# The last 64-row tile of FFN-down: two half passes of adjacent sums as 64-row tiles in the two halves of the array

## The chip, the cores and the metric

The kernel runs on one core of a Trainium2 chip. A core has TensorE (PE in the profile; its weight loads are PEld), VectorE (DVE), ScalarE (ACT), GpSimd (POOL) and SyncE (SP), which here only issues DMAs. The metric is device time in microseconds of one execution, the median of several.

## The reference

The inputs are x (2 x 4096 tokens x 640), two sets of small block weights, a gate vector and the weights of a gated feed-forward net. What is computed, in float32:

```python
g = sigmoid((x * gate_w).sum(-1, keepdims=True))
a = irfft(block_mlp(rfft(x, over the 4096 tokens)))   # complex, 4 blocks of 160, ReLU, soft shrinkage
b = (gelu(x @ w_gate) * (x @ w_up)) @ w_down          # 640 -> 1728 -> 640
out = g * a + (1 - g) * b
```

The change lies in the product with `w_down` (1728 x 640), called FFN-down here, at the end of the kernel.

## The kernel before

**Split numbers.** Operands of TensorE are in a float32 form that keeps fewer bits. To keep the accuracy, a value x is held as a high part (`high`, line 268, a ScalarE copy that rounds) and a low part (`low`, line 271, a VectorE subtraction x - high). A product of two split values is three passes: high x high, low x high and high x low; low x low is left out.

**The stages.** First come the gate and up products, with the forward transform put in between (to about 1440 us of the span), then the block MLP in the frequency domain, and last FFN-down with the inverse transform, from about 1883 us on. FFN-down goes in 32 steps. A step handles two tiles of 128 tokens, n1 and n2 (`toks`), and adds into them what `inv2` computes, 12 passes on line 287 (24 in a few steps).

**A step of FFN-down.** `down` (lines 1086 to 1132) computes the 2 x 2 block product of a pair of token tiles (rows) and two halves of the inner dimension (columns) with the four quarters of `w_down` in the Strassen-Winograd way, with seven products in place of eight. Each is called `blk(a_, b_)`: a11 x b11, s2 x t2, s3 x t3, s1 x t1, a12 x b21, a22 x t4, s4 x b22, in this order. An accumulator is a PSUM bank; A, E, B, C and Dd are different ones, A and E take two products each.

The inner dimension 1728 is 13.5 tiles of 128. Each half has seven tiles; in the second half the seventh (j == 6) has only 64 rows. The products whose left side comes from that half, or whose weights do, are listed in `HALF`. For these the last tile takes two passes, not three:

```python
ops += [(hh, wh), (hh, wl)] if j == 6 and a_ in HALF else [(hh, wh), (hl, wh), (hh, wl)]
```

Here rows 0 to 63 of `hh` hold the high part of the 64 rows and rows 64 to 127 their low part; `wh` holds the high part of the weights twice, so the first pass is high x high and low x high in one. `wl` holds the low part of the weights in rows 0 to 63 and zeros in rows 64 to 127, so the second pass is high x low with half of its rows idle. A step has 4 products of 21 passes and 3 of 20, 144 in all, each with a load of 128 columns of weights (the stationary side is the left operand, `ho`) and a stream of 320 columns. All of them are on line 458 (`run`).

**Preparing the operands.** `h_op` (line 1046) makes the split left side `ho` of one product: ScalarE copies the first five tiles (128x640) and the last two (128x256), VectorE subtracts. For a name in `HALF` the subtraction of the last two is a 128x128 and a 64x128, the latter written to rows 64 to 127. `down` calls the functions in `hooks` between its products: hook k prepares, for k = 0 to 4, the left sides of s3, s1, a12, a22 and s4 of this step, two or more products ahead of their use, and hooks 5 and 6 those of a11 and s2 of the next. ScalarE writes a buffer again only when TensorE has read it. The sums on GpSimd (`h_s3`, `h_s2`, `h_s1`) and the loads for the next step are in the hooks too. The order on each engine is the program's order; nothing is rescheduled.

**Preparing the weights.** `wd_pre` computes the seven forms of the weights once, during the gate and up products; `form` splits each, stores it to DRAM (`wdf`), and `wd_load` brings it back for FFN-down.

Of the kernel before, what the change touches and what calls it, by code (L numbers as in the profile page):

```python
# [10 lines left out]
F32 = mybir.dt.float32  # L11
# [4 lines left out]
P = 128  # L16
# [196 lines left out]
def spectral_mix_kernel(ctx: ExitStack, tc: tile.TileContext, a):  # L213
    nc = tc.nc
    out = a["out"]

    def dr(t, off, ap):
        return bass.AP(tensor=t.tensor, offset=t.offset + off, ap=ap)
# [7 lines left out]
    def bank():  # L226
        return psum.tile([P, 512], F32, name="bank", tag="bank")

    def big(shape, dt=F32, name="big"):
        return pool.tile(shape, dt, name=name, tag="big", bufs=18)  # L230
# [4 lines left out]
    def small(shape, dt=F32, name="small"):  # L235
        return pool.tile(shape, dt, name=name, tag="small", bufs=17)

    def tiny(shape, dt=F32, name="tiny"):
        return pool.tile(shape, dt, name=name, tag="tiny", bufs=21)
# [4 lines left out]
    def st(dst, src):  # L244
        late.append((dst, src))
# [21 lines left out]
    def high(dst, src, scale=1.0):  # L267
        nc.scalar.activation(dst, src, AF.Copy, scale=scale)  # L268

    def low(dst, src, hi, eng=nc.vector):  # L270
        eng.tensor_sub(dst, src, hi.bitcast(F32))  # L271

    def split(dst_h, dst_l, src, eng=nc.vector):

        high(dst_h, src)
        low(dst_l, src, dst_h, eng)
# [179 lines left out]
    def run(dst, ops, first=True):  # L456
        for i, (l, r) in enumerate(ops):
            nc.tensor.matmul(dst, l, r, start=first and i == 0, stop=i == len(ops) - 1, skip_group_check=True)  # L458
# [446 lines left out]

    V, WM, S2, HR, HO = {}, {}, {}, {}, {}
    HALF = ("a12", "a22", "s4", "b21", "t4", "b22")
    c_seq = [(b, na) for b in range(2) for na in range(16)]  # L910
# [10 lines left out]
    def wd_raw(t):  # L921
        raw = RAW["d", t] = small([P, D], name="draw")
        if t < NPAIR:
            ld(raw, a["wd"][t * P:(t + 1) * P])
        else:
            nc.gpsimd.memset(raw[64:], 0.0)
            ld(raw[:64], a["wd"][t * P:])
# [5 lines left out]
    def wd_pre(j):  # L933
        o = {}
        pair = (j, j + 6) if j < 6 else (12, 13)

        def loads():
            for t in pair:
                wd_raw(t)

        def sums(k):
            def f():
                if not o:
                    r1, r2 = (RAW.pop(("d", t)) for t in pair)
                    o.update(b11=r1[:, :320], b12=r1[:, 320:], b21=r2[:, :320], b22=r2[:, 320:])
                n, p, q = (("t1", "b12", "b11"), ("t2", "b22", "t1"), ("t3", "b22", "b12"), ("t4", "b21", "t2"))[k]
                if k % 2 == 0:
                    o["x"] = small([P, 2, 320], name="wx")
                o[n] = o["x"][:, k % 2]
                nc.vector.tensor_sub(o[n], o[p], o[q])  # L950
            return f

        def form(n):
            def f():
                w = small([P, 2, 320], F32R, name="wf")
                if j == 6 and n in HALF:
                    x = o[n][:64]
                    nc.gpsimd.memset(w[64:, 1].bitcast(F32), 0.0)
                    split(w[:64, 0], w[:64, 1], x)
                    high(w[64:, 0], x)  # L960
                else:
                    split(w[:, 0], w[:, 1], o[n])
                st(dr(wdf[j], 640 * FORMS.index(n), [[14 * 320, P], [1, 640]]),
                   w.rearrange("p h d -> p (h d)").bitcast(F32))
            return f
        return [loads], [sums(0), sums(1), form("t1"), form("b21")], [sums(2), sums(3), form("t2"), form("b11"),
                                                                      form("t3"), form("t4"), form("b22")]
# [78 lines left out]
    def h_op(i, name, eng=nc.vector):  # L1046
        t = big([P, 5, 2, P], F32R, name="ho")
        uh, ul = (tiny([P, 2, P], F32R, name="ho") for k in range(2))
        src, six = HR[i].pop(name) if name in ("s1", "s3", "s4", "a22") else HR[i][name]
        split(t[:, :, 0], t[:, :, 1], src, eng)  # L1050
        high(uh, six)
        if name in HALF:
            low(ul[:, 0], six[:, 0], uh[:, 0], eng)
            low(uh[64:, 1], six[:64, 1], uh[:64, 1], eng)
        else:
            low(ul, six, uh, eng)
        HO[i, name] = [(t[:, j, 0], t[:, j, 1]) for j in range(5)] + [(uh[:, j], ul[:, j]) for j in range(2)]

# [27 lines left out]
    def down(i, u, hooks):  # L1086
        b, na = c_seq[i]
        n1, n2 = toks(na)
        g1, g2 = gs[:, b, 1, n1:n1 + 1], gs[:, b, 1, n2:n2 + 1]
        u1, u2 = u[n1], u[n2]  # L1090
        c1, c2 = slice(0, 320), slice(320, 640)
        acc = lambda: bank()[:, :320]

        def blk(a_, b_):
            h = HO.pop((i, a_))
            ops = []
            for j, (hh, hl) in enumerate(h):
                wh, wl = WM[j][b_]
                ops += [(hh, wh), (hh, wl)] if j == 6 and a_ in HALF else [(hh, wh), (hl, wh), (hh, wl)]
            return ops  # L1100
        hooks[0]()
        e = small([P, 2, 320], name="e")
        A = acc()
        run(A, blk("a11", "b11"))
        nc.scalar.activation(e[:, 0], A, AF.Copy)
        hooks[1]()
        B = acc()
        run(B, blk("s2", "t2"))
        nc.vector.tensor_add(e[:, 0], B, e[:, 0])
        hooks[2]()  # L1110
        C = acc()
        run(C, blk("s3", "t3"))
        nc.vector.tensor_add(e[:, 1], C, e[:, 0])
        hooks[3]()
        E = acc()
        run(E, blk("s1", "t1"))
        for x in (E, e[:, 1]):
            nc.vector.scalar_tensor_tensor(u2[:, c2], x, g2, u2[:, c2], op0=OP.mult, op1=OP.add)
        hooks[4]()
        run(A, blk("a12", "b21"), first=False)  # L1120
        nc.vector.scalar_tensor_tensor(u1[:, c1], A, g1, u1[:, c1], op0=OP.mult, op1=OP.add)
        hooks[5]()
        Dd = acc()
        run(Dd, blk("a22", "t4"))
        nc.vector.tensor_add(e[:, 1], Dd, e[:, 1])
        nc.vector.scalar_tensor_tensor(u2[:, c1], e[:, 1], g2, u2[:, c1], op0=OP.mult, op1=OP.add)
        st(out[b, n2], u2)
        hooks[6]()
        run(E, blk("s4", "b22"), first=False)
        nc.vector.tensor_add(e[:, 0], E, e[:, 0])  # L1130
        nc.vector.scalar_tensor_tensor(u1[:, c2], e[:, 0], g1, u1[:, c2], op0=OP.mult, op1=OP.add)
        st(out[b, n1], u1)
# [66 lines left out]
    for k, (b, n2) in enumerate(a_seq):  # L1199
        i, j = steps_a[k]  # L1200
# [31 lines left out]
    for i, key in enumerate(keys):  # L1232
# [16 lines left out]
        for j, t in enumerate(quads):  # L1249
# [10 lines left out]
            n = len(late)  # L1260
# [27 lines left out]
    def events(i, j):  # L1288
        for f, *args in todo.get((i, j), []):
            f(*args)  # L1290
    wl = lambda part, *js: [(wd_load, j, part) for j in js]
# [9 lines left out]
           S - 3: [(v_load, 1), *wl(2, 2)],  # L1301
           S - 2: [(h_load, 0, 0), *wl(1, 2), (h_load, 0, 1), (wd_later,)],
           S - 1: [(c_split, 0), (h_op, 0, "a11"), *wl(1, 3, 4, 5), *wl(0, 6), (h_s3, 0, nc.gpsimd), (h_s2, 0, nc.gpsimd), (c_load, 1)],
           S: [(h_op, 0, "s2"), (c_split, 1), (h_s1, 0, nc.gpsimd)],
           S + 1: [*wl(2, 3), (flush,), *wl(2, 4), (wd_later,)]}
    for i in range(S + 2):
# [16 lines left out]
        if 0 <= i - 1 < S:  # L1323
            b, c, n = steps[i - 1]
# [8 lines left out]
    for i in range(len(c_seq)):  # L1333
        n = i + 1 if i + 1 < len(c_seq) else None
# [3 lines left out]
        def step(k):  # L1338
            def f():
                if (i, k) == (0, 0):  # L1340
                    wd_load(5, 2)
                    wd_later()
                if (i, k) == (0, 2):
                    ahead.update(inv2(1))
                if k in (0, 5):
                    flush()
                if k < 5:
                    if k == 0:
                        h_s4(i)
                    h_op(i, ("s3", "s1", "a12", "a22", "s4")[k])  # L1350
                if n is not None:
                    if k in (1, 2):
                        h_load(n, k - 1)
                    if k == 2 and n > 1:
                        c_load(n)
                        v_load(n)
                    if k == 4:
                        h_s3(n, nc.gpsimd)
                        h_s2(n, nc.gpsimd)
                    if k == 5:  # L1360
                        h_op(n, "a11")
                        if n > 1:
                            c_split(n)
                    if k == 6:
                        h_op(n, "s2")
                        h_s1(n, nc.gpsimd)
            return f
# [23 lines left out]
```

## Time and profile before

| | |
|---|---|
| median of 3 runs | 2622.28 us (2621.71 to 2625.66) |
| the profiled execution | 2621.81 us, span 2620.0 us |
| TensorE busy | 2601.1 us (99%) |
| VectorE, ScalarE, GpSimd busy | 2056.4, 1488.1, 378.2 us |
| passes of FFN-down (line 458, `bank<-wx,ho`) | 4608, busy 681.5 us |

Lines such as `L458 PE MATMUL bank<-wx,ho 128*128 128x320 f32 x4608 | 681.5, 309 | 0.0` name the source line, the engine, the operation, the tiles written and read, the rows and columns of the array in use (128*128), the shape of the stream, the count, the busy time in us, the mean length of one in ns, and the engine's idle time just before them with what ended it. Because matmuls overlap in the array, the length of one (309 ns) is more than the distance from one to the next. A row of a timeline holds the start, the length from the first start to the last end of a merged run, and in brackets the idle time before it with what ended it. A row of the windows view holds the stretch, its length, and for each engine the busy time with the count of instructions, then the granted clock of TensorE (1.00 is full), the share of the DMA engines and GB/s.

### The profile page before, as it was taken

The page shows a single profiled execution, that of the slowest core. Times are in us where ns is not written, and L with a number is a line of the kernel's source. Part 1 is how long each engine was busy: PE and PEld are TensorE (multiplying, and loading weights), DVE is VectorE, ACT ScalarE, POOL GpSimd, SP SyncE. Part 2 cuts the span into 40 slices and gives each one's busy share as a digit, 9 for nine tenths or more (in the row PEclk, how much of TensorE's full clock was granted, in tenths as well). Part 3 has the DMA queues.
Part 4 walks back from the last instruction along what each step waited for, and adds up shares of the span by engine and source line. Part 5 has one row for each costly group of instructions (what it writes and reads, how often), then busy time and mean ns, then how long its engine had stood idle before and what let it go on. Part 6 is the DMA issues. An engine that isn't in the chain of part 4 may idle for free. (4 is left out here: it accounts for less than half of the span.)

```text
span 2620.0 us, 54180 instructions
## 1 busy us (share of the span) xinstructions
PE 2601.1 (99%) x20308; PEld 2590.4 (99%) x20308; DVE 2056.4 (78%) x4223; ACT 1488.1 (57%) x3501; POOL 378.2 (14%) x377
## 2 busy tenths in 40 slices
PE   9999999999999999999999999999999999999999
PEld 9999999999999999999999999999999999999999
DVE  7656567777677777777756788787899999899998
ACT  5444445665555556666645777787744444444443
POOL 0000000000000000000002011111143333333332
PEclk9999999999999999999999999999999999999999
DMA  6454457676667577767766354457944444444442
GB/s 215 165 185 168 175 186 223 206 226 198 214 202 249 167 244 234 238 209 228 229 210 218 115 153 150 129 164 218 309 159 151 135 137 139 151 151 151 144 133 96
DMA packets 341659, 483.10 MB, mean 184 GB/s; under 512 B 24652, under 2 KB 214092, under 8 KB 341396
## 3 DMA queue, kind: packets, MB, share of 16 engines
q1 hardware_dynamic: 325844, 438.15, 52.9%
q0 software_dynamic: 15552, 41.49, 4.5%
q8 instruction: 160, 2.62, 0.4%
q14 instruction: 103, 0.84, 0.1%
HBM read 299.90 MB, written 179.64 MB: 183 GB/s over the span
## 5 line engine op out<-in xcount | busy, mean ns | idle before, releaser
L458 PE MATMUL bank<-xo,w 128*128 128x256 f32 x11736 | 1414.1, 281 | 8.8 <-ACT xo L268 4.9
L458 PEld LDWEIGHTS bank<-xo,w 128*128 128x128 f32 x11736 | 1402.3, 189 | 11.5 <-ACT xo L268 5.2
L458 PE MATMUL bank<-wx,ho 128*128 128x320 f32 x4608 | 681.5, 309 | 0.0
L458 PEld LDWEIGHTS bank<-wx,ho 128*128 128x128 f32 x4608 | 677.6, 188 | 0.0
L481 ACT ACTIVATE u<-bank 128x256 f32<-128x256 f32 x408 | 156.6, 384 | 330.6 <-PE bank L458 327.5
L271 DVE TENSOR_TENSOR ho<-hraw,ho 128x640 fp32r<-128x640 f32 (+3 forms) x384 | 281.2, 773 | 5.1 <-ACT ho L268 3.1
L523 DVE TENSOR_TENSOR u<-bank,u 128x256 f32<-128x256 f32 x204 | 86.2, 423 | 157.8 <-PE bank L458 156.3
L268 ACT ACTIVATE ho<-hraw 128x640 fp32r<-128x640 f32 x320 | 160.1, 571 | 64.7 <-PE bank L458 61.0
L271 DVE TENSOR_TENSOR xs<-xr,xs 64x640 fp32r<-64x640 f32 x128 | 105.0, 820 | 72.6 <-ACT xs L268 65.7
L271 DVE TENSOR_TENSOR xo<-xraw,xo 128x512 fp32r<-128x512 f32 x209 | 143.0, 685 | 24.0 <-ACT xo L268 22.4
L1081 ACT ACTIVATE uu<-bank,gs 128x320 f32<-128x320 f32 x120 | 54.8, 524 | 174.4 <-PE bank L287 172.1
L287 PE MATMUL bank<-wm,h 128*128 128x320 f32 (+1 forms) x816 | 142.4, 310 | 0.0
L482 ACT ACTIVATE h<-bank 128x256 f32<-128x256 f32 x204 | 77.7, 381 | 107.8 <-PE bank L458 102.0
L604 DVE TENSOR_TENSOR as<-bank,as 64x320 f32<-64x320 f32 x256 | 113.7, 483 | 28.5 <-ACT as L603 26.3
L268 ACT ACTIVATE xo<-xraw 128x512 fp32r<-128x512 f32 x209 | 129.1, 625 | 5.9 <-DMA xraw<-in_xT_dram 4.8
L1025 POOL TENSOR_TENSOR hraw<-hraw 128x640 f32<-128x640 f32 x64 | 88.3, 1395 | 263.2 <-DMA hraw<-hD 148.5
L287 PEld LDWEIGHTS bank<-wm,h 128*128 128x128 f32 (+1 forms) x816 | 120.9, 182 | 2.5
L555 POOL MEMSET h<- 64x512 f32 x16 | 8.3, 522 | 785.2 <-PE bank L458 316.3
L268 ACT ACTIVATE ho<-hs 128x640 fp32r<-128x640 f32 (+1 forms) x128 | 67.1, 571 | 83.9 <-PE bank L458 78.8
L271 DVE TENSOR_TENSOR s2s<-s,s2s 128x320 fp32r<-128x320 f32 x128 | 111.5, 929 | 0.0
L482 ACT ACTIVATE p<-p 128x256 f32<-128x256 f32 x204 | 84.4, 414 | 46.3 <-DVE p L505 45.4
L603 ACT ACTIVATE as<-bank 64x320 f32<-64x320 f32 x256 | 96.7, 426 | 20.1 <-PE bank L602 17.4
(139 smaller groups left out, 3486.2 us busy)
## 6 DMA issues: line engine op xcount, KB each, us to landing
xo<-xD SPq DMA_DIRECT2D x124, 512.0 KB
xraw<-in_xT_dram SPq DMA_DIRECT2D x225, 256.0 KB
hD<-h SPq DMA_DIRECT2D x224, 256.0 KB
hraw<-hD SPq DMA_DIRECT2D x128, 320.0 KB
xD<-xo POOLq DMA_DIRECT2D x64, 512.0 KB, 3.1
xr<-in_x_dram SPq DMA_DIRECT2D x64, 320.0 KB
scr<-as SPq DMA_DIRECT2D x64, 320.0 KB
sc<-scr SPq DMA_DIRECT2D x64, 320.0 KB
```

What stands on the lines that cost most here:

```text
L268: nc.scalar.activation(dst, src, AF.Copy, scale=scale)
L271: eng.tensor_sub(dst, src, hi.bitcast(F32))
L287: nc.tensor.matmul(dst, l, r, start=i == 0, stop=i == len(ops) - 1)
L458: nc.tensor.matmul(dst, l, r, start=first and i == 0, stop=i == len(ops) - 1, skip_group_check=True)
L481: copy = lambda d, s_: nc.scalar.activation(d, s_, AF.Copy)
L482: gelu = lambda d, s_: nc.scalar.activation(d, s_, AF.Gelu_apprx_tanh)
L523: nc.vector.tensor_add(u2, C, u2)
L555: nc.gpsimd.memset(h[64:], 0.0)
L603: nc.scalar.activation(stg[hi, cs], pa[lo, :320], AF.Copy)
L604: nc.vector.tensor_add(stg[hi, cs], pa[hi, :320], stg[hi, cs])
L1025: eng.tensor_sub(d["a21"][k], d["a11"][k], d["a21"][k])
L1081: nc.scalar.activation(uu[n2][:, cs], pe[:, :320], AF.Copy, scale=gs[:, b, 0, n2:n2 + 1])
```

## The change

The products a12 x b21 and a22 x t4 stand next to each other. The high x low pass of their 64-row tiles becomes a pass with 64 rows in each. For a12 it uses rows 0 to 63, as the last pass of the sum. For a22 it uses rows 64 to 127 and is moved to the front of the sum; the rest of a22's passes follow in the old order. So the two half passes are adjacent in TensorE's order. In the built program the first has the array tile of 64x128 at row 0, the second at row 64; all other down passes are 128x128.

For that, t4's low weights of tile 6 are put into rows 64 to 127 (zeros in 0 to 63), and a22's operand holds its high part in rows 64 to 127 and its low part in rows 0 to 63. The high part is also written to rows 0 to 63 of a spare tile, where the subtraction can read it: `h_op` for a22 has ScalarE copies of 128x128, 64x128 and 64x128 in place of one of 128x256. VectorE's subtractions keep their count and sizes. s4 x b22 keeps its full pass with the zeros.

```diff
             def f():
                 w = small([P, 2, 320], F32R, name="wf")
                 if j == 6 and n in HALF:
                     x = o[n][:64]
-                    nc.gpsimd.memset(w[64:, 1].bitcast(F32), 0.0)
-                    split(w[:64, 0], w[:64, 1], x)
+                    lo, zero = (slice(64, P), slice(0, 64)) if n == "t4" else (slice(0, 64), slice(64, P))
+                    nc.gpsimd.memset(w[zero, 1].bitcast(F32), 0.0)
+                    split(w[:64, 0], w[lo, 1], x)
                     high(w[64:, 0], x)
...
         split(t[:, :, 0], t[:, :, 1], src, eng)
-        high(uh, six)
-        if name in HALF:
+        if name == "a22":
+            high(uh[:, 0], six[:, 0])
+            high(ul[:64, 1], six[:64, 1])
+            high(uh[64:, 1], six[:64, 1])
+            low(ul[:, 0], six[:, 0], uh[:, 0], eng)
+            low(uh[:64, 1], six[:64, 1], ul[:64, 1], eng)
+        elif name in HALF:
+            high(uh, six)
             low(ul[:, 0], six[:, 0], uh[:, 0], eng)
             low(uh[64:, 1], six[:64, 1], uh[:64, 1], eng)
         else:
+            high(uh, six)
             low(ul, six, uh, eng)
...
                 wh, wl = WM[j][b_]
-                ops += [(hh, wh), (hh, wl)] if j == 6 and a_ in HALF else [(hh, wh), (hl, wh), (hh, wl)]
+                if j < 6 or a_ not in HALF:
+                    ops += [(hh, wh), (hl, wh), (hh, wl)]
+                elif a_ == "a22":
+                    ops = [(hh[64:], wl[64:]), *ops, (hh, wh)]
+                else:
+                    ops += [(hh, wh), (hh[:64], wl[:64]) if a_ == "a12" else (hh, wl)]
             return ops
```

## The prediction

> **What bounds the kernel now.** I read the page's first lines, then the stage that the change touches (the windows view from its second step to the start of its last), the groups of that stage by form, and its chain.
>
> ```profile
> span 2620.0 us, 54180 instructions
> PE 2601.1 (99%) x20308; PEld 2590.4 (99%) x20308; DVE 2056.4 (78%) x4223; ACT 1488.1 (57%) x3501; POOL 378.2 (14%) x377
> ```
> ```profile
> core 0: us, PE busy (x) PEld busy (x) DVE busy (x) ACT busy (x) POOL busy (x), PEclk, DMA share, GB/s
> 1905.54:2594.23 688.69, 688.69 (x4695) 688.69 (x4693) 654.88 (x1075) 317.86 (x690) 250.41 (x215) 1.00 0.45 145
> ```
> ```profile
> L458 PE MATMUL bank<-wx,ho 128*128 128x320 f32 x4608 | 681.5, 309 | 0.0
> L458 PEld LDWEIGHTS bank<-wx,ho 128*128 128x128 f32 x4608 | 677.6, 188 | 0.0
> ```
> ```profile
> 2203.40 21.13 PE bank L458 x144
> 2224.53 1.76 PE bank L287 x12
> 2226.29 21.15 PE bank L458 x144
> 2247.44 3.51 PE bank L287 x24
> ```
>
> Over 688.69 us of FFN-down TensorE is busy all 688.69 us at the full clock (1.00) and never idle; VectorE is busy 654.88 us (95%) and ScalarE 317.86 us (46%). So TensorE sets the time of this stage, with VectorE 5% behind it. A step is 144 down passes and 12 (once 24) passes of the inverse transform. The 144 passes take 21.15 us, so 0.147 us from one pass to the next, although the record of one lasts 0.309 us: passes overlap in the array's pipeline. What the change can be worth is therefore counted in passes of 0.147 us, 32 steps, straight off the span as long as VectorE keeps up.
>
> **The change, part by part.**
>
> *Passes.* In each step the sum a12 with b21 ends with a pass that multiplies the last 64 rows by the low half of the weights, and the sum a22 with t4 holds such a pass too. Both used 128 rows, of which 64 rows of weights were zero. Now the one uses rows 0 to 63 and ends its sum, the other uses rows 64 to 127, begins its sum, and follows it directly in TensorE's order; they write different banks. The count of passes stays 144. Nothing is removed; a gain comes only if the two halves overlap. If they coincide fully, one pass of 0.147 us goes per step: 32 x 0.147 = 4.7 us. If they do not overlap, nothing goes.
>
> Between these ends stand the weight loads, since each half still loads its own 128 columns. The trace shows how fast loads follow each other where matmuls are short, and when a load starts:
>
> ```profile
> 1458.91 1.01 PEld L742 LDWEIGHTS bank<-f,sc 128*128 128x128 f32 x8
> ```
> ```profile
> 1454.79 0.19 PEld L811 LDWEIGHTS bank<-z,wm 128*128 128x128 f32 x1
> 1454.91 0.14 PEld L812 LDWEIGHTS bank<-z,wm 128*64 128x64 f32 x1
> 1455.04 0.19 PEld L811 LDWEIGHTS bank<-z,wm 128*128 128x128 f32 x1
> ```
> ```profile
> 1454.91 0.28 PE L811 MATMUL bank<-z,wm 128*128 128x258 f32 x1
> 1455.03 0.28 PE L812 MATMUL bank<-z,wm 128*64 128x258 f32 x1
> 1455.15 0.28 PE L811 MATMUL bank<-z,wm 128*128 128x258 f32 x1
> 1455.27 0.28 PE L812 MATMUL bank<-z,wm 128*64 128x258 f32 x1
> 1455.39 0.29 PE L814 MATMUL bank<-zl,wl 128*128 128x258 f32 x1
> ```
>
> Eight loads in 1.01 us, the last lasting 0.19 us, are (1.01 - 0.19)/7 = 0.117 us each. The loads of L812 and of the second L811 start (1454.91, 1455.04) when the matmul before starts (1454.91, 1455.03): a load goes in as soon as the previous weights are taken over. If the two halves' weights can both be loaded beside the full pass ahead of them, they need 2 x 0.117 = 0.234 us from its start, where two full passes took 2 x 0.147 = 0.294 us until the second one began. The second half then starts 0.060 us sooner, and the next full pass 0.147 us after it. Gain 0.060 x 32 = 1.9 us. If the second load must instead wait for the first half's start, as every load in the trace does, it starts 0.147 us in, and the second half 0.117 us later, at 0.264 us: 0.030 us a step, 1.0 us. I take 1.9 us: the loads' own rate is the nearest row for two loads to separate rows, and 0 and 4.7 us are kept as ends.
>
> The Trainium skill, "TensorE: Matmul & The Clock Gate", Part 3 (Packing small matmuls), says that matmuls in different row groups run concurrently and start about 4 ns apart. By it the gain would be the full end of 4.7 us; no row here shows two row groups at once, and it speaks of starts once the weights are in, so it moves the end and not my value.
>
> *Preparing a22.* One ScalarE copy of 128x256 becomes a 128x128 and two 64x128; VectorE keeps its three subtractions at the same sizes.
>
> ```profile
> L268 ACT ACTIVATE ho<-hraw 128x256 fp32r<-128x256 f32 x160 | 65.0, 406 | 0.0
> L268 ACT ACTIVATE w<-wt 128x128 fp32r<-128x128 f32 x52 | 13.6, 298 | 0.1
> L840 ACT ACTIVATE hl<-hs 64x256 fp32r<-64x256 f32 x56 | 22.7, 406 | 0.0
> ```
>
> 64x256 costs what 128x256 does (406 ns), so 64x128 is set at the 298 ns of 128x128: 3 x 298 - 406 = 488 ns more a step, 15.6 us in 32 steps, all on ScalarE. What hides it is ScalarE's waits for buffers that TensorE frees:
>
> ```profile
> 2229.75 2.91 ACT L268 ACTIVATE ho<-hraw 128x640 fp32r<-128x640 f32 x6
> 2234.69 1.05 ACT L268 ACTIVATE ho<-hs 128x640 fp32r<-128x640 f32 x2 [2.03 <-PE bank L458]
> ```
> ```profile
> 2232.90 3.14 DVE L271 TENSOR_TENSOR ho<-hraw,ho 128x640 fp32r<-128x640 f32 x3
> 2236.08 0.49 DVE L1113 TENSOR_TENSOR e<-bank,e 128x320 f32<-128x320 f32 x1
> 2236.49 2.67 DVE L271 TENSOR_TENSOR ho<-hraw,ho 128x640 fp32r<-128x640 f32 x3
> ```
>
> The six ScalarE copies from 2229.75 are those of s1, a12 and a22; they end at 2232.66, and ScalarE then idles 2.03 us. 0.49 us fits in that. VectorE takes a22 up at 2236.49 and ends at 2239.16; its block is pass 105 of the step, 104 x 0.147 us after 2226.29, at 2241.6, so it is ready 2.4 us early. The new first pass needs only ScalarE's third copy, done by 2233.2. Cost on the path: 0; were the cover gone, 15.6 us. Behind the copies on ScalarE stand s4's, which wait for TensorE anyway.
>
> *The rest.* The zeros and the low half of t4's last tile change places in the weights' preparation, once, with the same instructions; DMAs, their queues and their order stay. 0.
>
> *Sum.* The profiled execution took 2621.81 us (span 2620.0), 0.47 us below the median of 2622.28 of the runs shown. 2621.81 - 1.9 = 2619.9; on the median, 2620.4 us. The whole effect is below the 0.2% (5.2 us) that a measurement of this kernel can tell from no change, and so is the largest possible gain of 4.7 us.
>
> **The rivals.**
>
> *Going from 128-row to 64-row passes and back stalls the array* (slower). The place: twice a step, before a12's last pass and after a22's first. If a pass in the other mode waits until the pass ahead has left the array, it starts 0.309 us after it and not 0.147: 0.162 us a change, 64 changes, 10.4 us; less the 1.9 us, +8.5 us, 2630.8 us. If its weights too are loaded only then, another 0.117 us each, 7.5 us: 2638.3 us. It decides from 0.030 us a change on, where it eats the 1.9 us. Against it: L811 and L812 alternate between 128 and 64 columns, and their matmuls stay 0.12 us apart in both directions. But those are columns; all the kernel's passes in the trace use more than 64 rows. The Trainium skill, "TensorEngine Tiling (Array Packing)", Key Properties, says that changing the tiling mode, not just the tile, drains TensorE. For 128x64, a mode in its list, the trace does not show that; for 64x128 no run here shows either.
>
> *The halves run one after the other.* For it: every load waits for the matmul before, and the compute order stays. Then each half is a full pass and the time stays 2622.3 us.
>
> *ScalarE's two more copies make VectorE late.* For it: VectorE is 95% busy here, and its queue is in order, so a late subtraction moves the ones that read sums out of the banks. Against it: the 2.03 us idle on ScalarE and the 2.4 us by which a22 is early. It decides when ScalarE is over 2 us behind; at worst the 15.6 us reach the path, 2636 us.
>
> **How the numbers follow.** Overlap of the halves, gain between 1.0 and 4.7 us, 0.44, and with it 2620.4 us. One after the other, 2622.3 us: 0.13. Stall at the change of mode 0.38, the lighter form 0.21 and the heavier 0.17: the column passes speak against it, but a change of rows is where nothing in the trace looks. Late VectorE: 0.05. The first two lie within 0.2%, from which 0.03 goes to a measurement that comes out below 2617.0, and to which a stall too small to tell adds 0.02: faster 0.03, same 0.56, slower 0.41. The range starts a little below the full overlap (2622.3 - 4.7 = 2617.6), at 2616.8, and runs through the lighter stall and just past the middle of the heavier (2638.3), to 2639; above it are left the upper part of the heavier stall and what a late VectorE could add to it, under 0.2 in all. The likeliest case alone spans 2617.6 to 2621.3.
>
> **What would show it.** Right: the 144 passes of a step go from 21.15 to about 21.09 us, the a22 half's matmul starts clearly less than 0.147 us after a12's last, and its load lies beside the pass before; TensorE still without idle time. The full overlap would show the two starts almost together and 21.00 us. A stall would show as more than 0.147 us ahead of the first half or behind the second, 21.4 us or more a step. Late preparation would show as idle time of TensorE before a22 or s4, released by ScalarE or VectorE. Wrong is the prediction above all if row halves do not behave as the column halves of L812 do.

## The result and the profile after

The changed kernel takes 2629.0 us (median, 2628.25 to 2630.78) where the kernel before took 2622.3 us: 6.7 us more, a ratio of 1.0026 with a 95% interval of 1.0016 to 1.0035. It is slower, by a little over what can be told from no change. The prediction of 2620.4 us was wrong in direction; its rival of a stall at the change between 128-row and 64-row passes is what happened.

The whole difference lies in FFN-down. The first fence has the weight loads of FFN-down in the kernel before, with their first and last start; the second has those of the changed kernel and, from its groups by form, its 128-row and 64-row passes and their loads.

```profile
L458 PEld LDWEIGHTS bank<-wx,ho x4608: 186/188/194, 1882.5 to 2615.1; 128*128 128x128 f32 x192
```
```profile
L458 PEld LDWEIGHTS bank<-wx,ho x4608: 182/188/195, 1883.8 to 2624.0; 128*128 128x128 f32 x192
...
L458 PE MATMUL bank<-wx,ho 128*128 128x320 f32 x4544 | 680.4, 310 | 0.0
L458 PEld LDWEIGHTS bank<-wx,ho 128*128 128x128 f32 x4544 | 668.1, 188 | 5.1 <-issue 5.1
...
L458 PE MATMUL bank<-wx,ho 64*128 64x320 f32 x64 | 13.3, 412 | 0.0
L458 PEld LDWEIGHTS bank<-wx,ho 64*128 64x128 f32 x64 | 6.0, 183 | 6.1 <-issue 6.1
```

From first to last load it was 732.6 us and is 740.2 us, 7.6 us or 0.24 us a step more. (Between the two profiled executions another 1.3 us lies before FFN-down. In the traces of the runs below its first load starts at 1882.3 to 1885.3 us, so this is spread; the medians differ by 6.7 us.) A 64-row load as such is no slower (183 ns against 188), but the 64-row loads have 6.1 us of idle time before them and the 128-row ones 5.1 us, both ended by "issue": the profile shows nothing that they wait for. Before, there was none.

The chain of waits of the changed kernel shows it by step; the prediction's rows had 21.13 and 21.15 us for the 144 passes:

```profile
2231.11 21.37 PE bank L458 x144
2252.49 3.51 PE bank L287 x24
2256.00 21.39 PE bank L458 x144
2277.39 1.76 PE bank L287 x12
2279.15 21.39 PE bank L458 x144
```

The 24 passes of the inverse transform are at 3.51 us as before. TensorE's busy time hides the difference, because the records of the passes cover it: in the windows view of the changed kernel PE is busy for all 740.00 us, and only PEld, at 728.83 us, shows that something waits (before, it was 732.65 of 732.70).

```profile
1884.00:2624.00 740.00, 740.00 (x4991) 728.83 (x4991) 652.94 (x1138) 347.68 (x792) 258.55 (x219) 1.00 0.44 144
```

Where the 0.23 us sit is seen in the weight loads around one pair (timeline of the changed kernel, weight loads alone):

```profile
2245.63 0.33 PEld L458 LDWEIGHTS bank<-wx,ho 128*128 128x128 f32 x2
2246.15 0.19 PEld L458 LDWEIGHTS bank<-wx,ho 64*128 64x128 f32 x2 [0.19 <-issue]
2246.50 0.59 PEld L458 LDWEIGHTS bank<-wx,ho 128*128 128x128 f32 x4 [0.16 <-issue]
```

The two 64-row loads lie in 0.19 us, although one of them takes 0.183: they start 3 to 4 ns apart, one on top of the other. In all 32 steps the two matmuls start 3 to 4 ns apart too. So the halves do overlap fully. But the loads of the pair start 0.38 us after the load before (2245.63 + 0.33 - 0.19 = 2245.77), where loads otherwise follow each other every 0.147 us, and the next 128-row load comes only 0.35 us after the pair's. Over the 32 steps, by the start times in the trace, the median from the last full matmul's start to the pair's is 0.237 us, from the pair's to the next full one's 0.343 us, and to the one after that 0.251 us. With the 0.003 us inside the pair these are 0.834 us for four intervals that took 4 x 0.147 = 0.588 us: 0.246 us a step, 7.9 us in all.

### The profile page after: what moved, and what is told of

It reads as the page before. It is cut to its first block, busy times and chain, and to the rows that moved or that the text cites. A ratio compares the mean times of both kernels' runs of the same rounds, so it can differ in the third digit from the quotient of the medians.

```text
span 2629.0 us, 54272 instructions
## 1 busy us (share of the span) xinstructions
PE 2609.7 (99%) x20308; PEld 2587.7 (98%) x20308; DVE 2023.6 (77%) x4223; ACT 1501.0 (57%) x3565; POOL 380.4 (14%) x377
## 5 line engine op out<-in xcount | busy, mean ns | idle before, releaser
L458 PE MATMUL bank<-wx,ho 128*128 128x320 f32 (+1 forms) x4608 | 689.2, 311 | 0.0
L458 PEld LDWEIGHTS bank<-wx,ho 128*128 128x128 f32 (+1 forms) x4608 | 674.1, 188 | 11.2 <-issue 11.2
L271 DVE TENSOR_TENSOR ho<-hraw,ho 128x640 fp32r<-128x640 f32 (+3 forms) x384 | 237.2, 666 | 4.2 <-ACT ho L268 3.2
L268 ACT ACTIVATE ho<-hraw 128x640 fp32r<-128x640 f32 (+3 forms) x384 | 173.0, 517 | 64.6 <-PE bank L458 61.0
```

## The experiments

The theory after this trace, called M below: every change between 128-row and 64-row passes costs TensorE about 0.19 us, in both directions, and the pair gives back one pass of 0.147 us. Two changes less one pass are 0.39 - 0.147 = 0.24 us a step. The rivals: the cost belongs to each 64-row pass (P); the two halves hinder each other (N); ScalarE's copies or the new order cost it (C); the first half waits for its bank (B).

### All passes on 128 rows again, with the changed operands

```diff
-                    ops = [(hh[64:], wl[64:]), *ops, (hh, wh)]
+                    ops = [(hh, wl), *ops, (hh, wh)]
                 else:
-                    ops += [(hh, wh), (hh[:64], wl[:64]) if a_ == "a12" else (hh, wl)]
+                    ops += [(hh, wh), (hh, wl)]
```

> The changed kernel's operands, copies and order (a22's high x low pass first), but both half passes use all 128 rows again, with zeros in the unused half; the output is the reference's. Theory M (a change between 128-row and 64-row passes costs about 0.19 us each, two a step, while the two halves coincide): no change is left, so 2622 us (2621 to 2624) and 0.147 us between all passes. Rival C (ScalarE's two more copies, or the new order of the a22 sum, cost the time): it stays at 2629 us.

Measured: 2623.0 us against 2622.2, ratio 1.0002 (0.9992 to 1.0011). Its chain has the old step:

```profile
2229.03 21.13 PE bank L458 x144
2250.16 3.51 PE bank L287 x24
```

The copies, the moved weights and the moved first pass cost nothing that can be told from 0; rival C falls. What remains of the change is the 64-row form alone.

### One half pass on 64 rows, the other on 128

a12's alone (rows 0 to 63):

```diff
-                    ops = [(hh[64:], wl[64:]), *ops, (hh, wh)]
+                    ops = [(hh, wl), *ops, (hh, wh)]
```

> Only a12's half pass uses 64 rows (0 to 63); a22's uses 128 rows, with zeros; the output is the reference's. Theory M: still two changes a step and no overlap, 32 x 2 x 0.19 = 12 us over before, 2634 us. Rival P (the cost belongs to each 64-row pass, about 0.18 us, and not to the change): one such pass, 32 x 0.18 = 5.7 us, 2628 us. Rival N (the two halves hinder each other as neighbours): no pair, 2622 us.

Measured: 2634.4 us, ratio 1.0044 (1.0029 to 1.0059). a22's alone (rows 64 to 127):

```diff
-                    ops += [(hh, wh), (hh[:64], wl[:64]) if a_ == "a12" else (hh, wl)]
+                    ops += [(hh, wh), (hh, wl)]
```

> Only a22's half pass uses 64 rows (64 to 127), a12's uses 128 rows, with zeros; the output is the reference's. Theory M: as with a12's alone, two changes a step and no overlap, 2634.4 us. If only one of the two positions in the array asks for the change, this one costs nothing (2622 us), or all of what the pair costs.

Measured: 2634.8 us, ratio 1.0043 (1.0028 to 1.0058). Both come out where M puts them (2634 and 2634.4 us) and 6 us above P's 2628. In the chain of the first a step takes 0.39 us more than 21.13 to 21.15, which is two changes of 0.195 us:

```profile
2210.72 21.52 PE bank L458 x144
2232.24 1.76 PE bank L287 x12
2234.00 21.54 PE bank L458 x144
```

A single 64-row pass is dearer than the pair by 5.4 us, so the pair's overlap is worth a pass of 0.147 us (4.7 us) as far as the spread tells. Rival N falls, and the position in the array makes no difference.

That a pass uses fewer rows than its neighbour is not enough for the cost. In the kernel before, passes with 66 rows stand among passes with 128; in the built program both have the array tile of 128x128. At 320 columns a 66-row pass starts 0.147 us after the 128-row pass ahead of it, and the next 128-row pass 0.149 us after it (medians of 128 and 93), and its loads have no idle time before them:

```profile
L287 PEld LDWEIGHTS bank<-wl,hl 66*128 66x128 f32 x128 | 24.1, 188 | 0.0
```

So it is the change between the array tiles of 128 and 64 rows that costs.

### Both on 64 rows, but 20 passes apart

```diff
-                    ops = [(hh[64:], wl[64:]), *ops, (hh, wh)]
+                    ops += [(hh, wh), (hh[64:], wl[64:])]
```

> Both half passes use 64 rows, but a22's stands at the end of its sum, 20 passes after a12's; the output is the reference's. Theory M: four changes a step and no overlap, 32 x 4 x 0.19 = 24 us, 2646 us. Rival P: two such passes, no overlap, 32 x 0.36 = 11.4 us, 2634 us. Rival N: 2622 us.

Measured: 2646.8 us, ratio 1.0093 (1.0076 to 1.011), 24.6 us over before. Four changes a step, no overlap: 32 x 4 x 0.19 = 24 us. The chain has 0.75 us more a step than 21.14:

```profile
2214.62 21.89 PE bank L458 x144
```

Rival P, at 2634 us, falls.

### The two halves in the other order

```diff
-        run(A, blk("a12", "b21"), first=False)
+        oa, od, Dd = blk("a12", "b21"), blk("a22", "t4"), acc()
+        for p in oa[:-1]:
+            nc.tensor.matmul(A, *p, start=False, stop=False, skip_group_check=True)
+        nc.tensor.matmul(Dd, *od[0], start=True, stop=False, skip_group_check=True)
+        nc.tensor.matmul(A, *oa[-1], start=False, stop=True, skip_group_check=True)
...
-        Dd = acc()
-        run(Dd, blk("a22", "t4"))
+        run(Dd, od[1:], first=False)
```

> The two half passes change places: a22's (rows 64 to 127, another bank than the pass before) first, a12's second; the output is the reference's. Theory M: the order of the halves doesn't matter, 2629 us, 0.237 us from the last full pass to the pair and 0.343 us from it to the next. Rival B (the first half waits because it adds into the bank that the full pass ahead still writes): the 0.09 us of waiting ahead of the pair's loads goes, 32 x 0.09 = 2.9 us, 2626 us.

Measured: 2630.8 us, ratio 1.0028 (1.0018 to 1.0038). The first half now writes another bank than the pass ahead of it, and the timeline (here each half has a line of its own) keeps its distances:

```profile
2244.62 0.60 PE L1136 MATMUL bank<-wx,ho 128*128 128x320 f32 x3
2245.15 0.41 PE L1137 MATMUL bank<-wx,ho 64*128 64x320 f32 x1
2245.15 0.41 PE L1138 MATMUL bank<-wx,ho 64*128 64x320 f32 x1
2245.49 0.57 PE L458 MATMUL bank<-wx,ho 128*128 128x320 f32 x2
```

The last of the three full passes starts at 2244.62 + 0.60 - 0.31 = 2244.91, the pair 0.24 us later, the next full pass 0.34 us after the pair. The time is 1.8 us above M's 2629, but FFN-down took only 0.3 us more in the trace than in the changed kernel's (740.45 us from first to last load, against 740.19). Rival B, at 2626 us, falls.

### Shorter passes inside and ahead of the pair

The pair on 160 columns:

```diff
-        run(A, blk("a12", "b21"), first=False)
+        oa, od, Dd = blk("a12", "b21"), blk("a22", "t4"), acc()
+        for p in oa[:-1]:
+            nc.tensor.matmul(A, *p, start=False, stop=False, skip_group_check=True)
+        for d, (l, r), k in ((A, oa[-1], 0), (Dd, od[0], 1)):
+            nc.tensor.matmul(d[:, :160], l, r[:, :160], start=k == 1, stop=k == 0, skip_group_check=True)
...
-        Dd = acc()
-        run(Dd, blk("a22", "t4"))
+        run(Dd, od[1:])
```

> The pair streams 160 columns in place of 320: half of a12's high x low of the last tile is left out, and what a22's half pass writes is overwritten by the next pass. If the array must run empty before the loads of the other kind start, the recorded 0.343 us from the pair to the next full pass falls by the 160 columns that are not streamed, 0.07 us, to about 0.27 us, and the time by 32 x 0.07 = 2.2 us, to 2626.8 us. If a change costs a fixed wait, it stays at 0.343 us and 2629 us.

The full pass ahead of the pair on 160 columns:

```diff
-        run(A, blk("a12", "b21"), first=False)
+        oa = blk("a12", "b21")
+        for k, (l, r) in enumerate(oa):
+            c = slice(0, 160 if k == len(oa) - 2 else 320)
+            nc.tensor.matmul(A[:, c], l, r[:, c], start=False, stop=k == len(oa) - 1, skip_group_check=True)
```

> The full pass right ahead of the pair streams 160 columns in place of 320 (half of high x high and low x high of a12's last tile is left out). If the array must run empty before the pair's loads start, the 0.237 us from that pass to them falls by about 0.07 us, to 0.167 us, and the time to 2626.8 us. If a change costs a fixed wait from the pass's start, it stays at 0.237 us and 2629 us.

Measured: 2627.5 us (ratio 1.0019, 1.0009 to 1.0028) and 2627.9 us (1.0020, 1.0010 to 1.0029). Both times lie 1.1 to 1.6 us below the changed kernel's, less than the 2.2 us expected and within the spread of the runs, so here the trace decides. From first to last load FFN-down takes 737.8 us in both, 2.4 us less than in the changed kernel: 32 times half of 0.147 us, as expected. Weight loads around the short pair, and then around the pair behind the short full pass (the row of L1137 holds the load of the short pass and that of a12's half):

```profile
2245.07 0.19 PEld L1138 LDWEIGHTS bank<-wx,ho 64*128 64x128 f32 x2 [0.19 <-issue]
2245.34 0.44 PEld L458 LDWEIGHTS bank<-wx,ho 128*128 128x128 f32 x3
```
```profile
2245.24 0.49 PEld L1137 LDWEIGHTS bank<-wx,ho 128*128 128x128 f32 x2
2245.56 0.18 PEld L458 LDWEIGHTS bank<-wx,ho 64*128 64x128 f32 x1
```

The next full pass comes 0.27 us after the pair (median 0.270) where it was 0.343; behind the short full pass, the pair comes after 0.166 us (median) where it was 0.237. Each interval shrinks by the 0.07 us of columns that are no longer streamed. So the wait is not a fixed time from a pass's start: it runs from the end of the stream. That splits a change in two. From the end of the stream until the loads of the other kind start it is 0.237 - 0.147 = 0.09 us. Then the load itself stands in the open: its matmul's record starts with it (in the trace of two pairs below, both stand at 2060.53), and the record is longer by the part of the load that nothing hides: 412 ns against 309, 0.10 us. The same 0.10 us is found where this is left behind, in the interval after the first full pass: 0.251 - 0.147 = 0.104 us. 0.09 + 0.10 = 0.19 us is a change, in both directions. What goes on in the array during the 0.09 us no run shows; that it has to run empty fits, since the wait counts from the end of the stream, and the load that otherwise lies beside the pass before does not.

### Two and three pairs between the same two changes

Two pairs:

```diff
-        run(A, blk("a12", "b21"), first=False)
+        oa, od, Dd = blk("a12", "b21"), blk("a22", "t4"), acc()
+        for p in oa[:-2]:
+            nc.tensor.matmul(A, *p, start=False, stop=False, skip_group_check=True)
+        for k, ((l, r), (l2, r2)) in enumerate(((oa[-2], od[-1]), (oa[-1], od[0]))):
+            nc.tensor.matmul(A, l[:64], r[:64], start=False, stop=k == 1, skip_group_check=True)
+            l2, r2 = (l2[64:], r2[64:]) if k == 0 else (l2, r2)
+            nc.tensor.matmul(Dd, l2, r2, start=k == 0, stop=False, skip_group_check=True)
...
-        Dd = acc()
-        run(Dd, blk("a22", "t4"))
+        run(Dd, od[1:-1], first=False)
```

> The full pass of the last tile is a 64-row pass too in a12 (rows 0 to 63) and a22 (rows 64 to 127): two pairs of 64-row passes stand side by side between the same two changes, and one pass time less is needed; low x high of the last tile is left out in both. Theory M: the second pair follows the first after 0.147 us and the changes cost what they did, 2629.0 - 32 x 0.147 = 2624.3 us. Rival P: four 64-row passes at 0.18 us, less two pass times of 0.147 us, 32 x 0.42 = 13.4 us over before, 2636 us, and the second pair comes 0.34 us after the first.

Measured: 2625.5 us, ratio 1.0011 (1.0002 to 1.0021), 1.2 us above M's figure and 10 us below P's. Matmuls and then weight loads around two pairs:

```profile
2060.00 0.60 PE L1136 MATMUL bank<-wx,ho 128*128 128x320 f32 x3
2060.53 0.41 PE L1138 MATMUL bank<-wx,ho 64*128 64x320 f32 x1
2060.53 0.41 PE L1140 MATMUL bank<-wx,ho 64*128 64x320 f32 x1
2060.78 0.30 PE L1138 MATMUL bank<-wx,ho 64*128 64x320 f32 x1
2060.78 0.31 PE L1140 MATMUL bank<-wx,ho 64*128 64x320 f32 x1
2061.02 0.70 PE L458 MATMUL bank<-wx,ho 128*128 128x320 f32 x3
```
```profile
2060.53 0.18 PEld L1138 LDWEIGHTS bank<-wx,ho 64*128 64x128 f32 x1 [0.19 <-issue]
2060.53 0.18 PEld L1140 LDWEIGHTS bank<-wx,ho 64*128 64x128 f32 x1
2060.63 0.19 PEld L1138 LDWEIGHTS bank<-wx,ho 64*128 64x128 f32 x1
2060.64 0.19 PEld L1140 LDWEIGHTS bank<-wx,ho 64*128 64x128 f32 x1
2061.02 0.59 PEld L458 LDWEIGHTS bank<-wx,ho 128*128 128x128 f32 x4 [0.19 <-issue]
```

The loads of the second pair start 0.10 us after those of the first, so beside its stream, and have no idle time ahead of them: between these 64-row passes loads go ahead as usual. Only the first pair's loads and the load after the last pair stand in the open. The second pair's matmuls start 0.25 us after the first's records, the 0.10 us of the open load and 0.147 us.

Three pairs, the same edit with tile 5's pass added (the slices and conditions of the other lines go one further):

```diff
-        for k, ((l, r), (l2, r2)) in enumerate(((oa[-2], od[-1]), (oa[-1], od[0]))):
+        for k, ((l, r), (l2, r2)) in enumerate(((oa[-3], od[-2]), (oa[-2], od[-1]), (oa[-1], od[0]))):
...
```

> Three pairs of 64-row passes between the two changes: besides the last tile's two passes, the high x low pass of tile 5 of a12 (rows 0 to 63) and of a22 (rows 64 to 127); left out are low x high of the last tile and half the rows of high x low of tile 5, in both sums. Theory M: one more pass time less than with two pairs, 2625.5 - 32 x 0.147 = 2620.8 us, just below the kernel before; three passes saved (0.441 us) pay the two changes (0.39 us). If further pairs cost more than 0.147 us each, it stays above 2622 us.

Measured: 2620.6 us against 2622.3, ratio 0.9995 (0.9986 to 1.0004). The figure is M's (2620.8); the interval holds 1, so for the whole kernel the sign is not shown, only that the loss is gone once three passes are saved. The kernel before has three half-empty passes in a step, which can save one and a half at most, so this form has nothing to pay its changes with; no version here that computes the whole result beats the kernel before.

FFN-down alone, from the first start to the last start of its weight loads in each trace, shows M without the spread of the other stages. The two kernels without 64-row passes agree there to within 0.05 us. The last column counts 0.194 us (0.09 + 0.104, from the changed kernel's intervals) for a change and 0.147 us for a pass saved, 32 times.

| | changes, passes saved in a step | us | over before | M |
|---|---|---|---|---|
| before | 0, 0 | 732.56 | | |
| all passes on 128 rows | 0, 0 | 732.52 | 0.0 | 0.0 |
| a12's half alone, a22's alone | 2, 0 | 744.98, 744.87 | 12.4, 12.3 | 12.4 |
| both, 20 passes apart | 4, 0 | 756.94 | 24.4 | 24.8 |
| changed kernel (one pair) | 2, 1 | 740.19 | 7.6 | 7.7 |
| two pairs | 2, 2 | 735.58 | 3.0 | 3.0 |
| three pairs | 2, 3 | 730.89 | -1.7 | -1.7 |

## Why the prediction was wrong

**What bounds it** was right: what was added on TensorE in FFN-down came out in the time, to within 1 us in every run, and TensorE waited for no operand there. But that its records leave no gap, as they do in both kernels, did not mean that it streamed all the time: the stall is inside the records.

**The overlap** was undersized. I let the two halves' loads follow each other at 0.117 us and got 0.060 us a step. The loads of the two row groups start 3 to 4 ns apart and lie on top of each other, and so do the matmuls: the whole pass of 0.147 us is gained, the upper end that I had kept. The Trainium skill, "TensorE: Matmul & The Clock Gate", Part 3 (Packing small matmuls), says that such matmuls start about 4 ns apart; the trace agrees with 3 to 4 ns.

**The passes around the pair** were the step that failed. I set them at their old distance of 0.147 us, so the two changes between 128 and 64 rows stood in the sum at nothing, and gave the stall 0.38. Measured, the pair comes 0.237 us after the full pass ahead, the next full pass 0.343 us after the pair, and the one behind it 0.251 us later. The evidence I held against it, the columns of L812, does not carry over: L811 and L812 go between 128 and 64 columns at 0.12 us a matmul, while going between 128 and 64 rows costs 0.195 us. The Trainium skill, "TensorEngine Tiling (Array Packing)", Key Properties, has that a change of the tiling mode drains TensorE. For rows the runs agree that a change makes TensorE wait (0.09 us from the end of the stream, and then 0.10 us of a load that is not hidden); for the tile of 128x64, which L812 has in the built program, the trace does not; the section gives no price. This rule should have weighed more than a neighbouring case.

**The size of the stall** in the rival was off in both terms. I took the wait as the record's length less the spacing, 0.309 - 0.147 = 0.162 us; measured it is 0.09 us: the pair starts 0.237 us after the full pass ahead, before that pass's record of 0.309 us has ended. The open load I took at 0.117 us; it is 0.10 us. So a change is 0.195 us, between my lighter form (0.162) and the heavier (0.279). With 64 changes and the full overlap: 64 x 0.195 - 4.7 = 7.8 us, or 2630.1 us against a measured 2629.0; the lighter form had given 2630.8 us, close by luck: its change was too cheap and its overlap too small, two errors of opposite sign. That 2629.0 lies inside the range is owed to this rival, not to the sum.

**The preparation of a22** was right: the third form of the copy, 64x128, takes 302 ns (I had set 298), nothing of it reached the path, and the run with all passes on 128 rows measures the whole of it at 0.8 us, which cannot be told from 0.

## What to carry to other kernels

Count the changes between array tiles of 128 and 64 rows, not the passes: one excursion into 64 rows and back costs about 0.39 us here, which is 2.7 passes of 320 columns, and the overlap of one pair repays only one. By this count row packing pays where whole runs of passes are 64 rows deep, or where the half-empty passes of many sums can be put side by side, so that one excursion saves three passes or more; no run here goes beyond three, where the whole kernel's time came out even. A single pair in a dense stream of full passes was better left padded with zeros. And where a stall is named that no row of the trace can show, price it from the rows there are and give it weight, even if a similar-looking case runs without it. When a change may make the array wait, look at the distances between starts and at the idle time of the loads, not at TensorE's busy share.

## What had not been expected

VectorE got lighter (652.9 us busy in FFN-down, where it was 687.6) with the same count and sizes of instructions. Its 64x128 subtractions from `hraw` into `ho` took 1105 ns on average in the kernel before, 453 in the run with all passes on 128 rows and 334 in the changed kernel; the groups by form, before and then after:

```profile
L271 DVE TENSOR_TENSOR ho<-hraw,ho 64x128 fp32r<-64x128 f32 x64 | 70.7, 1105 | 2.0
```
```profile
L271 DVE TENSOR_TENSOR ho<-hraw,ho 64x128 fp32r<-64x128 f32 x64 | 21.4, 334 | 1.0
L271 DVE TENSOR_TENSOR ho<-hraw,ho 128x640 fp32r<-128x640 f32 x160 | 153.9, 962 | 3.2 <-ACT ho L268 3.2
```

Of the 64x128 and 128x128 subtractions in the kernel before, the 79 that lasted over 500 ns lay on average for 0.96 of their length beside a GpSimd operation, the other 49 for 0.17. In the changed kernel all 128 lie beside one for 0.51 of their length on average, where it was 0.65, while the 128x640 ones got longer (853 to 962 ns): 22 of the 160 lasted over 1000 ns, where 5 had, and the 22 lay for 0.93 of their length beside a GpSimd operation; the others took 818 ns in both. That the two engines hold each other up is thus likely, and that the shifted ScalarE copies moved the meeting; neither was tested by itself. As TensorE waited for no operand in FFN-down, it is not seen in the time.
